# Transposing the tokens of one more tile by DMA instead of on the matrix engine

## The chip, the cores and the metric

The kernel runs on one core of a Trainium2 chip. A core has a matrix engine (TensorE, PE in the profile; its weight loads are PEld), two engines for elementwise work (VectorE, DVE; ScalarE, ACT), GpSimd (POOL) and SyncE (SP), which here only issue DMA transfers, and 16 DMA engines that move the data. Engines run in parallel, each through its own instructions in order, and wait for one another by semaphores. The metric is the time of one execution on the device in microseconds (us), the median of several runs.

## The reference, cut to what matters

Attention over 4 sequences of 768 positions with 8 heads of 64, where each position sees the first 8 positions and the last 96, with a bias that falls linearly with distance; then a two-layer network with a squared ReLU over the 3072 positions.

```python
scores = scale * np.matmul(q, k.transpose(0, 1, 3, 2))
is_global = pos[None, :] < int(n_global)             # 8
is_local = (rel >= 0) & (rel < int(n_local))         # 96
keep = is_global | is_local
scores = scores + bias[None, :, :, :]                # -slope of the head * distance
scores = np.where(keep, scores, -1000000000.0)
a = np.exp(scores - np.max(scores, axis=-1, keepdims=True))
a = a / (np.sum(a, axis=-1, keepdims=True) + 1e-09)
attn = np.matmul(a, v)
# ...
x = attn.transpose(0, 2, 1, 3).reshape(B * S, H * D)   # 3072 x 512
h = x @ w_in                                           # 512 x 2048
r = np.maximum(h, 0.0)
out = (r * r) @ w_out                                  # 2048 x 512
```

## The kernel before

The 3072 positions are 24 tiles of 128 (index `j`), two tiles to a block (12 blocks, `blk`). For each tile: q and k are transposed (`qkT`), scores are formed on TensorE (`sc`), exponentiated on ScalarE (`exp`, into `esc`), multiplied by a table of bias and mask on VectorE (`mul`, into `at`), multiplied by v on TensorE (`pv`, into `po`, two groups of four heads), and divided by the row sum on VectorE (`norm`, into `x`). For each block: x is transposed (`xT`), multiplied by eight slices of the first weights (`s1`, into `hT`), passed through ReLU on ScalarE (`relu`, into `hr`), squared on VectorE (`sq`, into `hs`) and multiplied by the second weights (`s2`, into `acc`).

The network work of some blocks is laid between the attention work of later tiles. A planner in the kernel's Python decides the order: every operation is given engines, an estimated cost, what it depends on and a priority (`key`), and the planner lists them in the order in which they would start. The program on each engine is this list. `SHIFT`, `LEADS` and `STEP` are tables of numbers that move single operations: `LEADS` moves a whole tile, `SHIFT` one kind of operation, for all tiles or for one, and `STEP` ties a tile's scores to a certain `s1` step.

The tokens of a tile are transposed in one of two ways. For tiles below `JX` it is four TensorE transposes into PSUM and a copy on VectorE or ScalarE; from `JX` on it is one DMA transpose that SyncE issues:

```python
JQK, JX = 6, 8
# ...
if j < JX:
    def emit_f(e, j=j):
        trx = ps_g.tile([P, KM, P], BF16, name="trx", tag="g")
        x = tiles["x", j].rearrange("p h d -> p (h d)")
        for kt in range(KM):                     # KM = 4
            nc.tensor.transpose(
                out=trx[:, kt, :], in_=x[:, kt * P : (kt + 1) * P], identity=ident
            )
        tiles["trx", j] = trx
    # ...
    def emit_xT(e, j=j, blk=blk, tt=tt):
        # ...
        any_copy(
            e, tiles["xT", blk][:, :, tt * P : (tt + 1) * P], tiles.pop(("trx", j))
        )
    # ...
else:
    def emit_xT(e, j=j, blk=blk, tt=tt):
        # ...
        nc.sync.dma_start_transpose(
            out=tiles["xT", blk][:, :, tt * P : (tt + 1) * P],
            in_=tiles["x", j].rearrange("p h d -> p (h d)"),
        )

    c = plan.op(("xT", j), {"SP": 1.2}, emit_xT, deps=norm, key=base + 5, takes=xT_ring)
    xop = xT_sp[j] = c
    c = plan.op(("xmoved", j), {"DMAQ": 0.9}, None, deps=[c])
```

q and k are transposed by DMA from tile `JQK` = 6 on, through the same SyncE queue as the transposes of x and the stores of the output. Their loads, issued by GpSimd, go into a ring of three buffers; the loads of tiles 8, 9 and 10 are held back by a small VectorE write to the buffer (a gate), so that they don't start too early. The gate of a tile is placed after the x transpose of the tile three before it, if that one is a DMA:

```python
if NFIRST + 2 + NQ - 1 <= j < JGATE:             # tiles 8 to 10
    def emit_gate(e, j=j):
        nc.vector.memset(qk_ring[slot(j)][:, :, :1], 0.0)

    gate = plan.op(
        ("gate", j), {"DVE": 0.07}, emit_gate, deps=qk_users[slot(j)] + [ld, xT_sp.get(j - 3)],
        key=base - 9,
    )
```

The first network weights come in eight slices of 256 columns. Slices 0 and 2 are loaded in two halves:

```python
TWO = (0, 2)
# ...
def load_w_in(s):
    n = 2 if s in TWO else 1
    for c in range(n):
        # ... one transfer of 256 / n columns
```

Of the kernel before, what the change touches and what calls it, by code (L numbers as in the profile page):

```python
# [21 lines left out]
class Plan:  # L22
# [8 lines left out]

    LAG = {"PE": 0.25, "ACT": 0.26, "DVE": 0.2, "SP": 0.6, "POOLQ": 0.8, "DMAQ": 1.2, "DMA": 0.0}
    URGE = 0.01
    SHIFT = {'T': 47, 'sc': -5.25, 'pv': -2, 'norm': 26.5, 'trx': -2, 'xT': 51, 'gk': 42, 'gv': -127.5, 'mul': 24, 'kl': 38.5, 'relu': 25.5, 'sq': 30, 's2': -5, 'o': 61, 'st': 78, ('mul', 3): 28, ('tr', 4): 10, ('xT', 5): -22, ('sc', 6): 14, ('pv', 7): -4, ('norm', 7): -17, ('trx', 7): -3, ('sc', 8): -12, ('pv', 8): -18, ('pv', 10): 45, ('sc', 11): 12, ('pv', 12): -50, ('sc', 13): 17, ('sc', 14): 6, ('pv', 14): 10, ('norm', 14): -28, ('sc', 15): -21, ('exp', 15): 20, ('exp', 16): 83, ('mul', 16): 92, ('norm', 16): -9, ('sc', 17): 32, ('pv', 17): 28, ('pv', 21): 9.5, ('pv', 22): -10, ('norm', 22): 8, ('s1', 2): -8.5, ('sq', 2): -10, ('relu', 3): 24, ('sq', 3): -82, ('s1', 5): 6, ('s1', 6): 30, ('sq', 6): 6, ('s1', 7): -6, ('sq', 7): -92, ('relu', 8): 40, ('s1', 9): -2, ('s1', 10): -10, ('s2', 0): 7.5, ('s2', 2): 1, ('s2', 4): -15, ('s2', 5): 37, ('s2', 6): -5, ('s2', 7): -3, ('s2', 9): 4.5, ('s2', 11): 30}

    def shift(self, name):
        early = name[-1 if name[0] in ("T", "tr") else 1]
        return self.SHIFT.get(name[0], 0.0) + self.SHIFT.get((name[0], early), 0.0)

# [65 lines left out]
def kernel(  # L105
# [35 lines left out]
    NFIRST = 4  # L141
    NSPLIT = 4
    NBIAS = 3
    JQK, JX = 6, 8
    NQ, NKT = 3, 2 * TPB
    NG = 8 - NACC
    G = ("g", NG)
# [7 lines left out]
    def const(shape, dt, name):  # L155
        return consts.tile(shape, dt, name=name, tag=name)
# [18 lines left out]
    pbt = const([P, 2, P], FP32, "pbt")  # L175
    pbw = const([P, 2, P], FP32, "pbw")
    plan = Plan()
    LEADS = {3: 51, 4: 17, 5: 16, 6: 27, 8: 2, 9: 20, 10: 42, 11: 47, 12: 0, 14: 0, 15: 7.5, 16: 34, 17: 46, 20: 28, 21: 15, 23: 56}
    SAFE = {j: 1.6 for j in range(6, 12)} | {14: 4.2, 15: 3.2, 16: 3.5}
    SAFEX = {9: 1.5, 11: 1.5, 13: 2.5}  # L180

# [2 lines left out]
    JOIN = {(7, 0), (12, 0), (21, 0), (16, 0), (23, 0), (18, 0), (20, 0), (15, 0)}  # L184
    COPY = [14, 15, 19, 20, 22]
    BEHIND = {}
    HOLD = ((10, 0),)
    STEP = {(4, 0): -7, (12, 0): 37, (5, 0): -2, (10, 0): 29, (13, 0): 30, (23, 1): 81}
    JGATE = 11
    NHS = 14  # L190
    NWARM = 8
# [13 lines left out]
    def slot(j):  # L205

        return j if j < NFIRST + 2 else NFIRST + 2 + j % NQ
# [60 lines left out]
    def emit_ones(e, js):  # L268
        for j in js:
            nc.vector.memset(v_sb[j][:, :, D : D + 1], 1.0)  # L270
# [38 lines left out]
    for g in range(NFIRST + 2, NT, 6):  # L309
        js = range(g, min(g + 6, NT))  # L310
        o = plan.op(
            ("ones", g), {"DVE": 0.2}, lambda e, js=js: emit_ones(e, js),
            key=-1.0, ready=15.0,
        )
# [40 lines left out]
    kl = [const([P, NPAIR, P], BF16, f"kl_{i}") for i in range(2 if COPY else 0)]  # L355
# [8 lines left out]
    for j in range(NT):  # L364
        b, t = divmod(j, TPB)
        first = t == 0
        need = 8 * (j // 2)
        base = need - LEADS.get(j, LEAD) + 4 * (j % 2)
        if (j, 0) in JOIN:
# [3 lines left out]
        if j in late:  # L373
            def emit_load(e, j=j):
                load_tile(j)
            gate = None
            if NFIRST + 2 + NQ - 1 <= j < JGATE:
# [8 lines that stand above are left out]
# [13 lines left out]
        for n in range(2) if j < JQK else ():  # L399
            users = []  # L400

            def emit_tr(e, j=j, n=n, fp=fp):
# [9 lines left out]
            tr = plan.op(  # L412
                ("tr", n, j), {"PE": 0.5 if fp else 0.24}, emit_tr,
                deps=[land["qk"[n], j]], key=base, takes=(*G, [users]),
            )
# [12 lines left out]
        if j >= JQK:  # L428
            def emit_dT(e, j=j, T_=T_):
# [5 lines left out]
            T = plan.op(  # L435
                ("T", j), {"SP": 1.3}, emit_dT,
                deps=[land["q", j], land["k", j], xT_op[j - 3]] + ku, key=base - 6,
            )
            T = plan.op(("moved", j), {"DMAQ": 1.2}, None, deps=[T])
            qk_users[slot(j)].append(T)  # L440
            if j in SAFE:

                T = plan.op(("seen", j), {"DMA": SAFE[j]}, None, deps=[T])
# [6 lines left out]
        mul, mul_users = {}, {}  # L450
# [55 lines left out]
        for gs in SETS.get(j, [tuple(range(groups))]):  # L506
            n = 8 * len(gs)
            sc_users = busers[2 * gs[0] : 2 * gs[-1] + 2]
            if (j, gs[0]) in JOIN:

                o, also, taken = joint
# [16 lines left out]
            if j < NBIAS:  # L528
# [6 lines left out]
            o = plan.op(  # L535
                ("sc", j, gs[0]), {"PE": 0.2 + 0.029 * n},
                lambda e, gs=also, f=emit_sc: f(e, gs), deps=[*deps, bias],
                key=base + 1 + 2 * gs[0], takes=takes,
            )
# [91 lines left out]
        norm = []  # L631
# [174 lines left out]
    for o in plan.ops:  # L806
        if o["name"][0] == "sc":
            j = o["name"][1]
            n = STEP.get(o["name"][1:], 4 * j - LEAD)
            if n >= 0 and j >= NFIRST:  # L810
                o["deps"].append(s1_ops[n // NSTEP, n % NSTEP])
                if o["name"][1:] in HOLD:
                    n += 1
                    s1_ops[n // NSTEP, n % NSTEP]["deps"].append(o)

    for blk in range(NBLK):
# [9 lines left out]
        for s, sub, half in order2:  # L826
# [5 lines left out]
            def emit_s2(e, blk=blk, s=s, sub=sub, half=half, w=w, cols=cols, own=own):  # L832
# [15 lines left out]
            o = plan.op(  # L848
                ("s2", blk, s, sub), {"PE": 0.43 * w / d_model}, emit_s2,
                deps=[d, land["wout", s]] + users[-1:],  # L850
                key=8 * blk + s + 2.0 + (0 if not last else 8 * sub + 8 * (half or 0)),
                takes=((*G, [users]) if own else ("acc", NACC, [users])) if s == 0 else None,
            )
# [6 lines left out]
            if s == NSTEP - 1:  # L860
# [14 lines left out]
                def emit_st(e, blk=blk, sub=sub, half=half, cols=cols):  # L875
# [9 lines left out]
                st = plan.op(  # L885
                    ("st", blk, sub), {"SP": 0.8 if (blk, sub) in HALVES else 0.4}, emit_st,
                    deps=[ev, s1_ops[NLATE, 0] if blk < NLATE - 2 else None],
                    key=8 * blk + s + 9.0,
                )
                st = plan.op(("stored", blk, sub), {"DMAQ": 1.4}, None, deps=[st])  # L890
# [40 lines left out]
```

The softmax here doesn't subtract the row's maximum and nothing guards it: scores larger than these inputs give would overflow.

## Time and profile before

| | before |
|---|---|
| time, median of three runs | 211.37 us (211.1 to 211.55) |
| span of the profiled execution | 209.3 us |
| granted TensorE clock | 1.0 |
| TensorE transposes of x (`trx`) | 32 matmuls, 8 tiles |
| copies of `trx` to `xT` | 5 on ScalarE, 3 on VectorE |
| DMA transposes of x | 16 |
| DMA transposes of q and k | 18 |

The profile numbers lines of the kernel: L709 is the TensorE transpose of x, L733 its DMA transpose, L430 the DMA transpose of q and k, L493 the scores, L646 `po`, L763 the first network layer (`hT`), L838 the second (`acc`), L880 the stores. Times in it are microseconds from the start of the span unless marked ns. A wait line names the engine and what it was about to do, then what released it, then the total, the number of waits and the longest. Matmuls are pipelined, so each one's duration overlaps the next one's; a few per cent of matmul records are missing from a trace.

### The profile page before, as it was taken

Reading aid. Unit: us, or ns where it says so; the run is one execution under the profiler, and the core shown is the slowest. Engines: PE = TensorE matmul, PEld = TensorE weight load, DVE = VectorE, ACT = ScalarE, POOL = GpSimd, SP = SyncE. Lnnn points to the kernel's source line nnn. Section 1 sums busy time; section 2 is a strip of 40 time slices with the busy share of each in tenths; the row PEclk is TensorE's granted clock in tenths of the full one; section 3 lists DMA queues with packets and bytes.
Section 4 is the critical chain, followed back from the end, with each engine's and each line's share of the span. In section 5 each row is a group of like instructions: output and inputs, shape, how many; then the busy total and the mean of one; then the engine's idle time right before and its main releaser. Section 6 shows DMA issues by size and latency. Waiting matters only on the chain.

```text
span 209.3 us, 4983 instructions
## 1 busy us (share of the span) xinstructions
PE 202.7 (97%) x1957; PEld 141.9 (68%) x1984; DVE 142.1 (68%) x370; ACT 120.2 (57%) x224; POOL 75.3 (36%) x93
## 2 busy tenths in 40 slices
PE   7998999999999999999999999999999999999994
PEld 3876887665756667676856676676676865865853
DVE  7699788523685787585958666676696865781730
ACT  6776588244872674654736564663575826841631
POOL 8999675541837057131455131313500000000000
PEclk9999999999999999999999999999999999999999
DMA  9999999999999999979999996969983421130402
GB/s 129 151 169 183 182 191 200 178 177 229 137 144 147 195 134 131 222 86 142 188 130 113 208 95 69 175 82 142 177 73 75 129 50 28 57 93 3 102 0 100
DMA packets 113705, 27.32 MB, mean 131 GB/s; under 512 B 105362, under 2 KB 110738, under 8 KB 113682
## 3 DMA queue, kind: packets, MB, share of 16 engines
q0 software_dynamic: 80256, 13.37, 85.5%
q1 hardware_dynamic: 33426, 13.64, 35.3%
q8 instruction: 15, 0.25, 0.5%
q14 instruction: 8, 0.07, 0.1%
HBM read 27.26 MB, written 6.29 MB: 160 GB/s over the span
## 4 chain that ended last, share of the span: by engine, by line
PE 88%; DVE 7%; issue 2%; ACT 2%
PE acc L838 38%; PE hT L763 37%; PE sc L493 5%; PE po L646 4%; DVE x L674 2%; PE warm L279 2%; PE tr L406 2%; ACT esc L559 1%; DVE hs L798 1%; DVE v L691 1%; DVE at L584 1%; PE trx L709 1%; DVE qkT L336 1%; DVE rs L673 1%; DVE E L343 0%
## 5 line engine op out<-in xcount | busy, mean ns | idle before, releaser
L763 PE MATMUL hT<-xT,win 128*128 128x256 bf16 x768 | 93.5, 273 | 0.4 <-DMA win<-in_moe_w_in_dram 0.4
L838 PE MATMUL acc<-wout,hs 128*128 128x512 bf16 (+2 forms) x373 | 87.1, 370 | 1.7 <-issue 0.3
L786 ACT ACTIVATE hr<-hT 128x512 f32<-128x512 f32 x96 | 57.4, 602 | 48.7 <-PE hT L763 42.9
L763 PEld LDWEIGHTS <-win 128*128 128x128 bf16 x768 | 72.8, 98 | 14.6 <-DMA win<-in_moe_w_in_dram 0.7
L798 DVE TENSOR_TENSOR hs<-hr 128x512 bf16<-128x512 f32 x96 | 64.7, 686 | 22.3 <-ACT hr L786 21.4
L838 PEld LDWEIGHTS <-hs 128*128 128x128 bf16 x400 | 36.8, 98 | 33.8
L559 ACT ACTIVATE esc<-sc 128x512 bf16<-128x512 f32 x78 | 39.9, 611 | 12.6 <-PE sc L493 12.6
L214 POOL DMA_DIRECT2D qk<-in_q_dram x23 | 20.9, 908 | 69.7 <-DMA qkT<-qk 54.8
L584 DVE TENSOR_TENSOR at<-esc,E 128x512 bf16<-128x512 bf16 x78 | 32.2, 422 | 10.4 <-ACT esc L559 7.6
L334 ACT COPY o<-acc 128x512 f32<-128x512 f32 (+2 forms) x21 | 11.6, 575 | 19.8 <-PE acc L838 19.8
L214 POOL DMA_DIRECT2D v<-in_v_dram x24 | 22.1, 922 | 1.0 <-DMA win<-in_moe_w_in_dram 0.6
L674 DVE TENSOR_TENSOR x<-po,rs 128x256 bf16<-128x256 f32 x48 | 20.4, 424 | 1.7
L214 POOL DMA_DIRECT2D qk<-in_k_dram x23 | 20.7, 911 | 0.5 <-DMA win<-in_moe_w_in_dram 0.5
L646 PEld LDWEIGHTS <-at 128*128 128x128 bf16 x352 | 15.8, 98 | 4.8 <-DVE at L584 0.2
L646 PE MATMUL po<-v,at 128*128 128x65 bf16 x352 | 17.6, 193 | 0.1
L673 DVE RECIPROCAL rs<-po 128x4 f32<-128x4 f32 x48 | 8.5, 176 | 10.8 <-PE po L646 10.3
L493 PEld LDWEIGHTS <-qkT 64*128 64x128 bf16 x312 | 9.4, 94 | 5.7 <-issue 4.9
L493 PE MATMUL sc<-qkT 64*128 64x128 bf16 x192 | 12.6, 218 | 0.0
L493 PE MATMUL sc<-qkT,qkT 64*128 64x128 bf16 x120 | 8.5, 216 | 0.0
L214 POOL DMA_DIRECT2D win<-in_moe_w_in_dram x10 | 8.1, 864 | 0.3 <-issue 0.2
L336 DVE COPY o<-acc 128x512 f32<-128x512 f32 x4 | 2.8, 692 | 6.2 <-PE acc L838 6.2
L214 POOL DMA_DIRECT2D wout<-in_moe_w_out_dram x8 | 6.0, 746 | 2.1 <-DMA win<-in_moe_w_in_dram 1.8
(45 smaller groups left out, 70.2 us busy)
## 6 DMA issues: line engine op xcount, KB each, us to landing
out_dram<-o SPq DMA_DIRECT2D x21, 256.0 KB, 3.2
v<-in_v_dram POOLq DMA_DIRECT2D x24, 128.0 KB, 5.9
qk<-in_q_dram POOLq DMA_DIRECT2D x23, 128.0 KB, 4.7
qk<-in_k_dram POOLq DMA_DIRECT2D x23, 128.0 KB, 5.3
wout<-in_moe_w_out_dram POOLq DMA_DIRECT2D x8, 256.0 KB, 9.1
win<-in_moe_w_in_dram POOLq DMA_DIRECT2D x6, 256.0 KB, 8.1
win<-in_moe_w_in_dram POOLq DMA_DIRECT2D x4, 128.0 KB, 5.1
out_dram<-o SPq DMA_DIRECT2D x4, 128.0 KB, 2.4
```

The lines of the kernel that those rows point to most:

```text
L214: nc.gpsimd.dma_start(out=dst, in_=src)
L334: nc.scalar.copy(dst, src)
L493: nc.tensor.matmul(out=tiles["sc", j, odd, g][:, at, :], lhsT=left[j - 1][half, pair, :] if kt else qkT[j % NKT][half, 1, pair, :], rhs=qk ...
L559: nc.scalar.activation(out=esc, in_=tiles.pop(("sc", j, odd, g)).rearrange("p a c -> p (a c)"), func=Act.Exp, scale=scale,)
L584: nc.vector.tensor_mul(at, tiles.pop(("esc", j, odd, g)), bias)
L646: nc.tensor.matmul(out=po[:, hi, :], lhsT=tiles["at", j, odd, g][:, at * P : (at + 1) * P], rhs=v_sb[kj][:, h, :], start=(i == 0), stop=(i ...
L673: nc.vector.reciprocal(rs, po[:, :, D : D + 1])
L674: nc.vector.tensor_tensor(out=x[:, 4 * hf : 4 * hf + 4, :], in0=po[:, :, :D], in1=rs.to_broadcast([P, 4, D]), op=Alu.mult,)
L763: nc.tensor.matmul(out=hT[:, c, :], lhsT=w_in_sb[s][:, kt, c * P : (c + 1) * P], rhs=tiles["xT", blk][:, kt, :], start=(kt == 0), stop=(kt ...
L786: nc.scalar.activation(hr, tiles.pop(("hT", blk, s)), Act.Relu)
L798: nc.vector.tensor_mul(hs, hr, hr)
L838: nc.tensor.matmul(out=tiles["acc", blk, sub, half], lhsT=hs[:, c, sub * P : (sub + 1) * P], rhs=w_out_sb[s][:, c, cols], start=(s == 0 an ...
```

## The change

Tile 7 joins the tiles whose x is transposed by DMA: `JX` goes from 8 to 7. Tile 7 is the second of block 3. The aim is to take its four transposes off TensorE and its copy off ScalarE. With this the numbers that place the operations of tiles 6 to 17 and the network blocks beside them are set anew, so that the order suits the other transpose. `TWO` is the same before and after. The loads of GpSimd keep their order.

```diff
-    SHIFT = {'T': 47, 'sc': -5.25, ... ('xT', 5): -22, ('sc', 6): 14, ('pv', 7): -4, ('norm', 7): -17, ...}
+    SHIFT = {'T': 47.0, 'sc': -5.25, ... ('xT', 5): -22.0, ('T', 6): -28.0, ('sc', 6): 6.0, ('mul', 6): -0.5, ('pv', 6): -20.5, ('norm', 6): 8.5, ...}
     # cut: some 110 entries for single operations of tiles 6 to 15 and blocks 3 to 7
...
-    JQK, JX = 6, 8
+    JQK, JX = 6, 7
...
-    LEADS = {3: 51, 4: 17, 5: 16, 6: 27, 8: 2, 9: 20, 10: 42, 11: 47, 12: 0, 14: 0, 15: 7.5, 16: 34, ...}
+    LEADS = {3: 51, 4: 17, 5: 16, 6: 49.5, 8: 140.0, 9: 30.0, 10: 27.0, 11: 48.0, 12: 14.0, 14: 0, 15: -25.5, 16: 34, ..., 7: 46.5, 13: 0.0}
...
-    HOLD = ((10, 0),)
-    STEP = {(4, 0): -7, (12, 0): 37, (5, 0): -2, (10, 0): 29, (13, 0): 30, (23, 1): 81}
+    HOLD = ((23, 1),)
+    STEP = {(4, 0): -7, (12, 0): 37, (5, 0): -2, (10, 0): 25, (13, 0): 39, (23, 1): 81, (6, 0): 17, (8, 0): 18, (9, 0): 27, (11, 0): 25, (14, 0): 35, (15, 1): 54}
```

`HOLD` names scores that the next `s1` step has to wait for in the plan.

In the programs that come out, the first 40 us of every engine are the same instructions in the same order, and so is TensorE's order after block 7. Between, the scores of tile 6 and 7 come one pair of `acc` matmuls earlier; the scores of tiles 8 to 11 come later among the network steps; the `po` groups and the network steps are moved around them. In SyncE's queue the first transpose of q and k goes ahead of the first store of the output, and tile 7's x goes between tile 8's and tile 9's transposes of q and k.

More of the change, by code (lines that the diff above doesn't have):

```diff
@@ L33 @@
     URGE = 0.01
-    SHIFT = {'T': 47, 'sc': -5.25, 'pv': -2, 'norm': 26.5, 'trx': -2, 'xT': 51, 'gk': 42, 'gv': -127.5, 'mul': 24, 'kl': 38.5, 'relu': 25.5, 'sq': 30, 's2': -5, 'o': 61, 'st': 78, ('mul', 3): 28, ('tr', 4): 10, ('xT', 5): -22, ('sc', 6): 14, ('pv', 7): -4, ('norm', 7): -17, ('trx', 7): -3, ('sc', 8): -12, ('pv', 8): -18, ('pv', 10): 45, ('sc', 11): 12, ('pv', 12): -50, ('sc', 13): 17, ('sc', 14): 6, ('pv', 14): 10, ('norm', 14): -28, ('sc', 15): -21, ('exp', 15): 20, ('exp', 16): 83, ('mul', 16): 92, ('norm', 16): -9, ('sc', 17): 32, ('pv', 17): 28, ('pv', 21): 9.5, ('pv', 22): -10, ('norm', 22): 8, ('s1', 2): -8.5, ('sq', 2): -10, ('relu', 3): 24, ('sq', 3): -82, ('s1', 5): 6, ('s1', 6): 30, ('sq', 6): 6, ('s1', 7): -6, ('sq', 7): -92, ('relu', 8): 40, ('s1', 9): -2, ('s1', 10): -10, ('s2', 0): 7.5, ('s2', 2): 1, ('s2', 4): -15, ('s2', 5): 37, ('s2', 6): -5, ('s2', 7): -3, ('s2', 9): 4.5, ('s2', 11): 30}
+    SHIFT = {'T': 47.0, 'sc': -5.25, 'pv': -2.0, 'norm': 26.5, 'trx': -2.0, 'xT': 51.0, 'gk': 42.0, 'gv': -127.5, 'mul': 24.0, 'kl': 38.5, 'relu': 25.5, 'sq': 30.0, 's2': -5.0, 'o': 61.0, 'st': 78.0, ('mul', 3): 28.0, ('tr', 4): 10.0, ('xT', 5): -22.0, ('T', 6): -28.0, ('sc', 6): 6.0, ('mul', 6): -0.5, ('pv', 6): -20.5, ('norm', 6): 8.5, ('trx', 6): 11.5, ('T', 7): 6.0, ('exp', 7): -2.0, ('gk', 7): 41.0, ('pv', 7): 24.5, ('norm', 7): 1.5, ('xT', 7): 1.0, ('gate', 8): -8.5, ('T', 8): 7.0, ('sc', 8): 3.0, ('exp', 8): -24.0, ('mul', 8): -1.0, ('gk', 8): 1.0, ('pv', 8): 127.0, ('norm', 8): 5.0, ('gv', 8): 4.5, ('xT', 8): -0.5, ('gate', 9): -6.0, ('T', 9): -6.5, ('sc', 9): -6.5, ('exp', 9): 6.0, ('gk', 9): 0.5, ('pv', 9): 5.5, ('norm', 9): 6.0, ('gv', 9): -4.5, ('xT', 9): 8.0, ('T', 10): -12.5, ('sc', 10): 3.0, ('mul', 10): -8.5, ('gk', 10): 1.0, ('pv', 10): -1.0, ('norm', 10): -5.0, ('gv', 10): -3.0, ('xT', 10): -0.5, ('T', 11): 3.5, ('sc', 11): -13.0, ('exp', 11): -10.5, ('mul', 11): -8.0, ('pv', 11): -8.0, ('norm', 11): -3.0, ('xT', 11): -5.5, ('T', 12): 1.5, ('exp', 12): -7.5, ('mul', 12): -13.0, ('pv', 12): -6.0, ('norm', 12): -0.5, ('xT', 12): 0.5, ('T', 13): -6.5, ('sc', 13): -3.0, ('exp', 13): 7.5, ('mul', 13): 0.5, ('gk', 13): -6.5, ('pv', 13): -19.5, ('norm', 13): -2.0, ('gv', 13): 13.0, ('T', 14): -9.0, ('sc', 14): 8.0, ('exp', 14): 11.5, ('mul', 14): -1.5, ('pv', 14): -28.0, ('gv', 14): 0.5, ('xT', 14): -13.5, ('T', 15): -1.5, ('sc', 15): -5.5, ('mul', 15): -11.5, ('kl', 15): -7.0, ('pv', 15): -24.5, ('norm', 15): -9.5, ('gv', 15): 3.0, ('xT', 15): -11.0, ('exp', 16): 83.0, ('mul', 16): 92.0, ('norm', 16): -9.0, ('sc', 17): 32.0, ('pv', 17): 28.0, ('pv', 21): 9.5, ('pv', 22): -10.0, ('norm', 22): 8.0, ('s1', 2): -8.5, ('sq', 2): -10.0, ('s1', 3): -3.5, ('relu', 3): 3.5, ('relu', 4): 11.5, ('sq', 4): 67.5, ('s1', 5): -7.5, ('relu', 5): 4.5, ('sq', 5): -8.0, ('s1', 6): 2.5, ('relu', 6): -6.0, ('sq', 6): 7.5, ('s1', 7): 4.5, ('relu', 7): 8.0, ('sq', 7): -54.0, ('relu', 8): 40.0, ('s1', 9): -2.0, ('s1', 10): -10.0, ('s2', 0): 7.5, ('s2', 2): 1.0, ('s2', 3): -2.0, ('o', 3): 6.0, ('st', 3): -0.5, ('s2', 4): -32.5, ('o', 4): 6.0, ('s2', 5): 18.5, ('o', 5): -15.0, ('st', 5): 19.5, ('s2', 6): 13.5, ('o', 6): -13.0, ('st', 6): -6.0, ('s2', 7): 6.5, ('st', 7): -8.5, ('s2', 9): 4.5, ('s2', 11): 30.0}
@@ L177 @@
     plan = Plan()
-    LEADS = {3: 51, 4: 17, 5: 16, 6: 27, 8: 2, 9: 20, 10: 42, 11: 47, 12: 0, 14: 0, 15: 7.5, 16: 34, 17: 46, 20: 28, 21: 15, 23: 56}
+    LEADS = {3: 51, 4: 17, 5: 16, 6: 49.5, 8: 140.0, 9: 30.0, 10: 27.0, 11: 48.0, 12: 14.0, 14: 0, 15: -25.5, 16: 34, 17: 46, 20: 28, 21: 15, 23: 56, 7: 46.5, 13: 0.0}
     SAFE = {j: 1.6 for j in range(6, 12)} | {14: 4.2, 15: 3.2, 16: 3.5}
```

## The prediction

> **What bounds the kernel now.** I read, in order: engine busy time on the page, then TensorE's waits, then busy time in four stretches after the start-up, then the chain of waits, and last the DMA transposes. The page's first part says who is full:
>
> ```profile
> span 209.3 us, 4983 instructions
> ...
> PE 202.7 (97%) x1957; PEld 141.9 (68%) x1984; DVE 142.1 (68%) x370; ACT 120.2 (57%) x224; POOL 75.3 (36%) x93
> ```
>
> TensorE is 97% busy and the next engine 68%. A pipelined matmul's duration overlaps its neighbour, so 97% is not proof; who waits is better evidence. TensorE's own waits:
>
> ```profile
> PE warm L279 <- DVE zero L267: 1.2, 1, 1.2
> PE hT L763 <- DMA win<-in_moe_w_in_dram: 0.4, 1, 0.4
> PE acc L838 <- issue: 0.3, 2, 0.2
> PE trx L709 <- DVE x L674: 0.3, 1, 0.3
> PE acc L838 <- DVE hs L798: 0.2, 1, 0.2
> PE acc L838 <- DVE qkT L620: 0.2, 1, 0.2
> ```
>
> Total, times, longest. 2.6 us in all, and the three largest fall before 20 us. By stretches (length, then PE, PEld, DVE, ACT, POOL busy):
>
> ```profile
> 20.00:50.00 30.00, 29.74 (x278) 21.96 (x283) 20.01 (x42) 17.42 (x32) 16.61 (x21) 1.00 1.72 186
> 50.00:100.00 50.00, 49.21 (x490) 33.38 (x497) 34.84 (x89) 29.40 (x56) 21.05 (x24) 1.00 1.65 154
> 100.00:150.00 50.00, 49.63 (x464) 34.63 (x469) 35.85 (x85) 28.66 (x52) 18.42 (x21) 1.00 1.29 138
> 150.00:206.50 56.50, 56.07 (x517) 39.17 (x522) 34.38 (x77) 30.00 (x55) 0.00 (x0) 1.00 0.35 66
> ```
>
> From 20 us to 206.5 us TensorE is idle for 186.5 - 184.65 = 1.85 us. Even that is mostly not idleness: the program has 400 matmuls into `acc`, the page's group has 373, and each of the 27 unrecorded ones leaves a hole of about 0.05 us ("issue" in the chain of waits below). 27 x 0.05 = 1.4 us, which leaves about 0.5 us of real waiting in 186 us. The order of this kernel has no slack left on TensorE: only fewer or cheaper TensorE instructions can shorten the middle, and any new wait lengthens it one for one.
>
> ```profile
> 57.44 0.22 PE trx L709 x4
> 57.66 0.24 PE po L646 x8
> 57.90 0.05 issue
> 57.96 0.38 PE acc L838
> 58.33 0.24 PE po L646 x8
> 58.58 1.29 PE acc L838 x6
> 59.87 0.22 PE trx L709 x4
> 60.10 0.55 PE sc L493 x16
> ```
>
> Start, length, what; this is the chain of waits around tiles 6 and 7. The second `trx` line is the work the change removes: tile 7's four transposes take 0.22 us of a full TensorE. What replaces it is a DMA transpose like those of tiles 8 to 23:
>
> ```profile
> L733 SPq DMA_TRANSPOSE xT<-x x16: 1188/1190/1211, 65.0 to 184.0; - x16
> ...
> DMA to landing us min/median/max: 2.4/2.6/4.9
> ```
>
> 1.19 us is the queue's issue time; landing takes 2.4 to 4.9 us. Asked transfer by transfer, those before 115 us, beside the loads, took 4.9, 3.8, 2.4, 4.2, 3.8 and 4.3 us; those from 132 to 150 us 2.4 to 2.7.
>
> **What the Trainium skill says.** "VectorE: DVE Perf Modes", section "The three transpose paths", gives 390 ns on TensorE and 1309 ns by DMA for one 128x128 bf16 block. The trace disagrees on what counts: one transpose shows 219 ns, but four in a stream advance TensorE by 0.22 us together, and the DMA moves four blocks with 1.19 us of issue and 2.6 us to landing. So the saving is four blocks at about 56 ns, not at 390. That 56 ns matches "TensorE: Matmul & The Clock Gate", section "Back-to-back issue gap", N/2.4 + 2.5 ns, for N = 128; the page also gives 81 ns for a sustained stream, which this trace doesn't show. "Trainium Kernel Development and Optimization", section "Key Constraints", says that DMAs issued by SyncE and GpSimd share the same 16 engines; the stretched landings beside loads agree. "Perfetto Trace Analysis", section "Identifying the Most-Contended Engine", warns against TensorE busy share as a measure; hence the waits above.
>
> **The change part by part.**
> (1) Removed: four transposes and their weight loads on TensorE, -0.22 us on the path. Also one 128x512 PSUM-to-SBUF copy on ScalarE (mean 583 ns in its group), at 57% busy: nothing on the path.
> (2) Added: one DMA transpose in SyncE's queue. No engine time; what matters is whether it lands in time.
> (3) Reordered: from TensorE's `acc` matmuls just before tile 6's scores, near 52 us, to block 7, near 130 us, instructions move by up to 2 us; later the two orders agree again. The number of separate runs of score matmuls is what could cost TensorE: entering or leaving one costs about 0.1 us (8 scores alone take 0.33 us in the chain of waits, 16 take 0.55, 24 take 0.78, so 0.028 us each and 0.1 us for the rest). Both programs have 21 such runs: 0 us. GpSimd's order of loads is the same.
> (4) Weights in halves: the first and third slices are already halved before; the text of the change names a condition, not an edit. 0 us.
> Sum: -0.22 us, plus new waits.
>
> **New waits.** I laid out the changed TensorE order at the spacings of the trace before (eight `hT` 0.87 us, two `acc` 0.43, eight `po` 0.24, scores as in (3)), and compared consumers with producers.
> - Tile 7's x. Its last `po` group should start at 57.7 us. For tile 9 before, x was ready for its DMA 1.1 us after that point (in the timeline, `po` 72.81, DMA 73.93). So the new DMA goes at 58.8, lands between 61.2 and 63.7 us; block 3's first matmul is due at 64.2. Margin 0.5 to 3.0 us: no wait, unless the SyncE queue is held by the store ahead of it, due at about 57.5.
> - Tile 9's q and k transpose now queues behind it: issued near 60.5, landing in up to 7.4 us (the longest before) by 68; its scores move from 68.6 to 70.0. No wait.
> - Tile 15's x: its last `po` group moves from 122.0 to 124.0 us, block 7 stays at 129.5. DMA at 125.1 (1.1 us after, as before: 122.0, 123.1), landing 127.5 to 129.4 with the latencies seen before 115 us, against 127.5 to 127.8 with those after 132. Margin 0.1 to 2.0 us: the tightest place. A wait of 0 to 0.5 us is possible here.
> - Others (tiles 8 to 14, 16, 17) keep distances from scores to `po` (2.7 us at least in both) and from `po` to the block's first matmul (4.7 us or more from DMA issue to use).
> I allow 0.1 us for new waits: 211.37 - 0.22 + 0.1 = 211.2 us.
>
> **Rivals.**
> - The DMA transposes collide. Tile 7's shares the DMA engines with the tail of tile 11's load (issued 55.3 to 57.9 us, about 5 us to land), tile 9's transpose and the load of tile 10, which its gate now releases about 1 us earlier. Between 36 and 72 us the engines are nearly saturated on the page (nines almost throughout). For it: `qkT` transposes there took up to 7.2 us. Against it: margins above were computed with those figures. If it bites, block 3 waits 1 to 2 us and, TensorE being full, the end moves by as much: 212 to 213.
> - TensorE transposes are hidden anyway and nothing changes. Against it: no idle time to hide them in. It would give 211.4.
> - VectorE or ScalarE becomes late, because the new order puts softmax work of two tiles close together (six exponentials in a row, about 0.5 us each, in both kernels). Some tens of 0.1 us waits would sum to 0.3 to 1 us: 211.5 to 212.2. For it: VectorE runs close behind ScalarE in that part, and a PSUM bank freed late stalls TensorE. Against it: it is so before as well, without waits.
> - More than the transposes is won, if small waits before vanish: at most the 0.5 us above, 210.7.
>
> **Range and chances.** The three runs before span 0.45 us, so a gain of 0.2 us barely shows. Downward the floor is 210.7 by the last rival; upward one missed landing costs about 1 us. Hence 210.9 to 212.2. Faster by 2% needs 4.2 us, more than TensorE's whole real idle time with the start and tail: 0.01. Slower by 2% needs several missed landings: 0.03. Within 2%: 0.96.
>
> **What would show it right or wrong.** In the profile after: 28 `trx` matmuls instead of 32, 17 DMA transposes of x, TensorE's waits after 20 us still at some tenths. A line among TensorE's waits of `hT` on the DMA `xT<-x` near 64 or 129 us would mean the landings were underestimated; waits of `sc` on `qkT<-qk`, that the queue order is at fault; waits of `po` on VectorE's `at`, that the softmax order is. The prediction is wrong if such waits sum to over 1 us, or if TensorE's saving is not about 0.2 us.

## The result, and the profile after

| | before | after |
|---|---|---|
| time, median | 211.37 us (211.1 to 211.89, 6 runs) | 212.62 us (212.13 to 213.47, 6 runs) |
| after / before | | 1.0062 [1.0035, 1.0088] |
| span of the profiled execution | 209.3 us | 210.5 us |
| end of TensorE's last matmul | 206.49 us | 207.20 us |

The change makes the kernel slower by 1.25 us; predicted was 211.2 us. The first part of the page:

```profile
span 210.5 us, 5005 instructions
...
PE 203.8 (97%) x1980; PEld 140.4 (67%) x1980; DVE 140.9 (67%) x368; ACT 121.3 (58%) x225; POOL 75.3 (36%) x93
```

TensorE's waits (total, times, longest) have one line that lies behind the start and that before doesn't have, the second:

```profile
PE warm L279 <- DVE zero L267: 1.2, 1, 1.2
PE hT L763 <- DMA xT<-x: 0.6, 1, 0.6
PE hT L763 <- DMA win<-in_moe_w_in_dram: 0.6, 2, 0.3
PE tr L406 <- DMA plain<-in_k_dram: 0.5, 1, 0.5
PE tr L406 <- DMA qk<-in_k_dram: 0.2, 1, 0.2
```

The first matmul of a network block waits for a DMA transpose of x; it is the sign that the prediction named for underestimated landings. The three below it are the loads at the start, which vary from run to run in both kernels. By stretches (length, then PE, PEld, DVE, ACT, POOL busy):

```profile
20.00:50.00 30.00, 30.00 (x282) 21.73 (x281) 18.70 (x40) 16.93 (x32) 16.72 (x21) 1.00 1.68 183
50.00:100.00 50.00, 49.35 (x492) 32.43 (x491) 35.55 (x89) 30.71 (x57) 21.03 (x24) 1.00 1.54 153
100.00:150.00 50.00, 50.00 (x469) 35.03 (x468) 34.56 (x79) 28.21 (x51) 15.79 (x18) 1.00 1.32 132
150.00:207.20 57.20, 57.20 (x526) 39.36 (x524) 35.03 (x79) 30.20 (x56) 2.63 (x3) 1.00 0.37 75
```

This trace has all 400 `acc` matmuls, so TensorE shows as full, apart from 0.65 us in the second stretch: the wait. The chain of waits there (start, length, what) names the tile:

```profile
58.30 0.19 DVE rs L673
58.50 0.02 issue
58.52 0.43 DVE x L674
58.95 0.02 SPq L733
58.98 0.03 issue
59.01 6.13 DMA xT<-x
65.14 0.04 issue
65.18 1.05 PE hT L763 x8
```

The DMA is tile 7's. Its x is ready at 58.95 us, SyncE issues at once, and 6.13 us later block 3 starts. Its eight matmuls then take 1.05 us instead of 0.87. The wait of 0.65 us and these 0.18 us together put TensorE 0.8 us later from there on than its order alone would.

The second loss lies at the very end. The last line of the chain of waits of before, and of after (start, length, what):

```profile
206.53 0.27 ACT o L334
```

```profile
207.24 0.27 ACT o L334
```

This is ScalarE's copy of the last result. From its end to the end of the span it is 209.317 - 206.792 = 2.525 us before, and 210.457 - 207.503 = 2.954 us after: 0.43 us more, in which no engine computes. The instructions of that stretch are the same in both.

### The profile page after: what moved, and what is told of

The parts are those of the page before. It is cut to its first block, busy times and chain, and to the rows that moved or that the text cites. A ratio compares the mean times of both kernels' runs of the same rounds, so it can differ in the third digit from the quotient of the medians.

```text
span 210.5 us, 5005 instructions
## 1 busy us (share of the span) xinstructions
PE 203.8 (97%) x1980; PEld 140.4 (67%) x1980; DVE 140.9 (67%) x368; ACT 121.3 (58%) x225; POOL 75.3 (36%) x93
## 4 chain that ended last, share of the span: by engine, by line
PE 84%; POOL 6%; DMA 6%; DVE 2%; issue 0%; ACT 0%; POOLq 0%; SPq 0%
PE hT L763 38%; PE acc L838 37%; PE sc L493 4%; PE po L646 4%; DMA xT<-x 3%; DMA win<-in_moe_w_in_dram 3%; POOL qk L214 3%; POOL win L214 2%; POOL v L214 2%; DVE x L674 1%; PE tr L406 0%; DVE at L584 0%; DVE hs L798 0%; DVE rs L673 0%; PE trx L709 0%
## 5 line engine op out<-in xcount | busy, mean ns | idle before, releaser
L838 PE MATMUL acc<-wout,hs 128*128 128x512 bf16 (+2 forms) x400 | 91.9, 371 | 0.0
L334 ACT COPY o<-acc 128x512 f32<-128x512 f32 (+2 forms) x23 | 12.7, 573 | 18.7 <-PE acc L838 18.4
L620 DVE COPY qkT<-qkT 128x32 bf16<-128x32 bf16 x11 | 3.3, 299 | 4.9 <-PE sc L493 4.8
```

The source lines that it names most:

```text
L334: nc.scalar.copy(dst, src)
L838: nc.tensor.matmul(out=tiles["acc", blk, sub, half], lhsT=hs[:, c, sub * P : (sub + 1) * P], rhs=w_out_sb[s][:, c, cols], start=(s == 0 an ...
```

## The experiments

Theories: A, tile 7's x lands late (A1: because tile 11's load is still in flight; A2: because of something else, such as the transpose of tile 9's q and k behind it); a rival, that something else in the new order costs time, in particular that SyncE issues the first transpose of q and k before the first store (C). Two more came from the runs: transposes of q and k land too late for the scores in the new order, in places that vary; and the longer end. Ratios are to runs of before on the same chip, with their 95% intervals; they leave out single runs that were over 1.5% slower than the fastest of their kernel, which the medians in us keep, and e17's profiled execution, which was one of them, is left out of the table and the sums below.

**e1: block 3 starts later.** `SAFEX` tells the planner how long after its DMA an x is usable; tile 7 gets an entry, and block 3's first step moves 1.3 us back in the order (as a side effect, two scores come 0.9 us earlier).

```diff
-    SAFEX = {9: 1.5, 11: 1.5, 13: 2.5}
+    SAFEX = {7: 2.5, 9: 1.5, 11: 1.5, 13: 2.5}
```

> The changed kernel with one planning number more (2.5 us of extra landing time for tile 7's x), which puts block 3's first matmuls 1.3 us later and the rest as it was; the DMA transpose stays. Theory A (the added time is TensorE's wait at about 64 us for tile 7's x, whose DMA took 6 us to land): the wait of hT on the DMA xT<-x shrinks to 0.2 us or less, the time falls to 211.2 to 211.6, ratio 0.999 to 1.001. Theory B (the new order of tiles 6 to 17 itself is the slower one): the order is nearly the same, so it stays at 212.3 to 212.9, ratio 1.005.

Measured: 211.84 us, ratio 1.0013 [0.9987, 1.0038]; no wait for x. Most of the excess is gone with the transposes' number unchanged, as A expects, though the later kernels with this edit keep more (below). Its profile does lose 0.23 us at 52.5 us, where tile 7's scores wait for their q and k.

**e2: the new order with the old transposes**, and **e3: the old order with the DMA transpose.**

```diff
-    JQK, JX = 6, 7     # e2: changed kernel
+    JQK, JX = 6, 8
-    JQK, JX = 6, 8     # e3: kernel before
+    JQK, JX = 6, 7
```

> The changed kernel's planning numbers, but tile 7 transposed on TensorE as before. Theory A: no wait of 0.5 us or more on a transpose of x before 100 us, TensorE does 0.22 us more, time 211.3 to 211.7 (ratio 0.9995 to 1.0015). Theory B (order): 212.3 or more, with waits on VectorE, ScalarE or the q and k transposes.

Measured: 222.13 us, ratio 1.0498 [1.0458, 1.0537], with waits in many places (`hT` on `xT` 2.5 us, `po` on `at` 1.6, `sc` on `qkT` 1.2).

> The kernel before with the one edit that tile 7's x goes by DMA, no new planning numbers. Block 3's first matmul stays due near 65.5 us. Theory A: the DMA is issued near 59.3 and lands by 65.4 if it again takes 6 us, so TensorE waits 0 to 0.3 us, time 211.1 to 211.6. If a DMA transpose of tile 7 costs something else (contention that delays other tiles' q, k or x), 212 or more with waits of sc on qkT<-qk.

Measured: 216.18 us, ratio 1.0232 [1.0183, 1.028]; tile 7's x causes no wait, but one of 1.4 us for the x of another tile near 129 us and others between 138 and 143 us do. Neither run splits the change into halves as meant: with the other transpose the planner lists everything behind it differently, and numbers searched for one form don't fit the other. They show only that `JX` can't be changed without a new search.

**e4: tile 11's load moved away.** A fourth tile gets the gate, so the load doesn't start before its buffer's last reader is further on.

```diff
-    JGATE = 11
+    JGATE = 12
```

> The changed kernel with a gate also for the load of tile 11, so that this load no longer runs when tile 7's x is transposed; block 3's first matmul stays due near 64.2 us. Theory A1 (the landing is stretched by the loads in flight): the DMA lands within 4 us of its issue, no wait at 64 us, time 211.1 to 211.8 unless the later load makes tile 11 wait. Theory A2 (the landing is stretched by something else, such as the q and k transpose behind it): it still takes 5.5 to 6.5 us and TensorE waits 0.5 us or more, time 212.2 or more.

Measured: 218.22 us, ratio 1.0303 [1.0267, 1.034]; as a whole much worse. Its profile has new waits near 83 us and at 131 to 135 us, for VectorE and ScalarE; that they come from the later loads is likely but not shown. What it was for is in the trace between 54 and 66 us. GpSimd's issues of loads in the changed kernel (start, length, what):

```profile
55.47 0.88 POOL L214 DMA_DIRECT2D qk<-in_q_dram  x1 [0.75 <-DMA qkT<-qk]
56.33 0.88 POOL L214 DMA_DIRECT2D qk<-in_k_dram  x1
57.20 0.90 POOL L214 DMA_DIRECT2D v<-in_v_dram  x1
```

and in e4:

```profile
53.65 0.88 POOL L214 DMA_DIRECT2D qk<-in_k_dram  x1
54.51 0.90 POOL L214 DMA_DIRECT2D v<-in_v_dram  x1
61.35 0.88 POOL L214 DMA_DIRECT2D qk<-in_q_dram  x1 [5.94 <-DVE qkT L620]
```

In the changed kernel three loads are issued in the 3.5 us before tile 7's transpose (59.01 us), in e4 the nearest is 5.2 us before it (59.70) and the next after it. The transpose ends with 32 packets of 4 bytes in the DMA records, its completion writes. In the changed kernel they come from 61.40 to 64.53 us, 2.4 to 5.5 us after the issue; in e4 all from 61.67 to 61.82, 2.0 to 2.1 us after it, and block 3 doesn't wait. The issues around the two are otherwise alike: in both, the store ahead was issued 2.52 us before and tile 9's transpose 1.3 to 1.4 us after, so A2 falls for that one. A1 holds for this place, by one profile of each: with no load in flight the transpose is done in 2 us, with the rest of a load it took 3.4 us more. In the profiles of the changed order (after, and below e6, e8, e14 and e16), all with that load close by, the last completion write came 3.5 to 5.5 us after the issue; how close the load is doesn't alone decide where in that range.

The Trainium skill, "DMA: Bandwidth & Descriptors", section "Queues, rings and completion order", says that a semaphore increment lands only after every earlier write of the same DMA engine, across its queues. No run here shows whether this delays the transpose: the records don't say which DMA engine moved a packet. It can't be all, since the data came late too: the 512 packets of 256 bytes that follow the issue moved from 1.8 to 4.5 us after it in the changed kernel, from 1.2 to 1.9 us in e4.

**e5, e6, e7: the store and the first transpose change places** in SyncE's queue: in e1's kernel, in the changed kernel, and, the other way round, in the kernel before.

```diff
-    ('T', 6): -28.0    # e5 (with e1's edit) and e6; e7 adds ('T', 6): -75 to before
+    ('T', 6): 20.0
```

> The kernel of e1 with one more swap, in SyncE's queue alone: the first store of the output goes ahead of the q and k transpose of tile 6 again, as in the kernel before. Theory C (the change has a second cost: the store between the transposes of tiles 6 and 7 lets tile 7's q and k land up to 1.25 us too late for its scores at 52 us): the tile 7 transpose is issued near 45.0 us instead of 45.6 to 46.1, no wait of sc at 52 us, the time falls by another 0.1 to 0.5 us against e1, to 211.2 to 211.6, at or just below the kernel before. Theory D (the late x was all): equal to e1, within 0.2 us.

> The changed kernel with that swap alone; block 3's first matmul stays due near 64.2 us. Theory C: the wait for tile 7's x at 64 us stays (0.4 to 0.9 us), the late q and k go: 0.1 to 0.6 us below the changed kernel on the same chip. Theory D: the same as the changed kernel.

> The kernel before with that swap in the other direction: tile 6's q and k transpose ahead of the first store, nothing else changed; tile 7 on TensorE. Its scores are 0.4 us later than in the changed kernel, so the margin is wider. Theory C: the transpose of tile 7 is issued at 45.6 to 46.1 us and lands by 51.4 to 53.6; some executions wait, median 0 to 0.4 us above the kernel before, with a wider spread. Theory D: no difference (ratio 0.999 to 1.001).

Measured: e5 212.55 us, ratio 1.0037 [1.0018, 1.0057]; e6 212.69, 1.0056 [1.0037, 1.0075]; e7 211.85, 1.0008 [0.9987, 1.0028]. C falls as the main cost: within the noise, 0.2 to 0.3%, the swap takes nothing from the changed kernel and adds nothing to before. What C names does occur, as one late landing among others: tile 7's q and k cost 0.23 us in e1's profile and 0.28 us in e14's. e6's profile shows no wait for tile 7's x, but one of 1.2 us of scores for `qkT` near 78 us: the loss isn't always in the same place.

**e8: the changed kernel once more**, to see what varies.

> The changed kernel itself, on the same chip as e5 to e7, so that they can be compared: ratio 1.003 to 1.008, spread over 1 us, with a wait for tile 7's x near 64 us that differs from the 0.65 us of its first profile by some tenths.

Measured: 212.75 us, ratio 1.005 [1.0018, 1.0082]. TensorE's waits for it:

```profile
PE sc L493 <- DMA qkT<-qk: 0.9, 1, 0.9
PE tr L406 <- DMA plain<-in_k_dram: 0.8, 1, 0.8
```

and its chain of waits from 71 us on:

```profile
71.07 8.84 DMA qkT<-qk
79.92 0.05 issue
79.96 0.62 PE sc L493 x16
```

The same kernel, but this time x is in time and the q and k transpose of tile 10 is not. It took 8.8 us. In the first profile it took 7.3 us from 70.31 and its scores started at 78.23, 0.6 us later; in before it took 7.2 from 67.39 and the scores came at 75.78, 1.2 us later. For tile 7 the distance shrank likewise from 1.4 to 0.9 us, for tile 13 from 5.0 to 0.5 us, of which 3.0 us are a longer landing (9.6 us instead of 6.6). These are the tiles whose scores can wait now.

**e9 to e12: later x, later scores of tile 10, both.** `SAFE` is for q and k what `SAFEX` is for x.

```diff
-    SAFE = {j: 1.6 for j in range(6, 12)} | {14: 4.2, 15: 3.2, 16: 3.5}
+    SAFE = {j: 1.6 for j in range(6, 12)} | {10: 3.5, 14: 4.2, 15: 3.2, 16: 3.5}   # e9, e10
     # e11: {10: 3.0, ...}; e12: {10: 2.6, ...}
-    SAFEX = {9: 1.5, 11: 1.5, 13: 2.5}
+    SAFEX = {7: 2.5, 9: 1.5, 11: 1.5, 13: 2.5}   # e9, e10, e12
     # e10 also: ('T', 6): 20.0, ('sc', 6): 14.0, the store first as in e6
```

> The changed kernel with two planning numbers more: block 3's first matmul 1.3 us later (as in e1) and tile 10's scores 0.9 us later than in the changed kernel (1.7 us later than in e1, which had moved them forward). The order of SyncE's queue is that of the changed kernel. Theory E (two landings are too late in the new order, both in the region of 60 to 80 us: tile 7's x at 64 us and tile 10's q and k at 77 us, which one bites differs from run to run): neither wait is seen in the profile; time 211.3 to 211.7, at most 0.1% above the kernel before, and the spread no wider than that of before. Theory A alone (only tile 7's x): equal to e12. If the excess sits elsewhere (start, end, tile 7's q and k): 212 or more.

> e9 with the first store of the output ahead of tile 6's q and k transpose, as in the kernel before. Theory C (late q and k of tile 7 at 52 us also cost): 0.1 to 0.4 us below e9, 211.2 to 211.5. Theory D (they do not): within 0.2 us of e9.

> The changed kernel with tile 10's scores 0.9 us later, and block 3's first matmul where it was (due at 64.2 us). Theory E: the wait at 77 us goes, that for tile 7's x at 64 us stays: 212.0 to 212.5, between e9 and the changed kernel (212.6 and 212.75). Theory A alone: no change, 212.6.

> The changed kernel with block 3's first matmul 1.3 us later and tile 10's scores where the changed kernel has them. Theory A alone: 211.3 to 211.7, as e9. Theory E: no wait for x at 64 us, but one of up to 1 us of sc on qkT<-qk near 77 us in some executions: 211.6 to 212.2.

Measured: e9 212.27 us, ratio 1.003 [1.001, 1.0049]; e10 212.24, 1.002 [1.0001, 1.0038]; e12 212.27, 1.0024 [1.0008, 1.004]; e11 213.65, 1.0104 [1.0076, 1.0131] (6 runs). e9 and e10 stay above what the theory of two late landings expected (at most 0.1%). The five kernels with later x (e1, e5, e9, e10, e12) keep 0.1 to 0.4%, on average 0.25%, whether the scores of tile 10 are moved or not; the changed kernel itself shows 0.4 to 0.6% (first result, e8, e17). The difference shows only over all of them: on one chip e5 and e8 agree within the noise. e11 is worse than expected. Its profile has the wait for tile 7's x (0.6 us) and 1.3 us of waits for the first weights at the start; the latter come before anything that the edit moves. With six runs, and after what e14 and e16 show below, it isn't evidence against later scores; it stays unexplained. e10's profile shows no late landing at all, TensorE's waits are those of the start:

```profile
PE warm L279 <- DVE zero L267: 1.2, 1, 1.2
PE tr L406 <- DMA qk<-in_k_dram: 0.3, 2, 0.2
PE hT L763 <- DMA win<-in_moe_w_in_dram: 0.3, 1, 0.3
PE trx L709 <- DVE x L674: 0.3, 1, 0.3
PE acc L838 <- DVE qkT L620: 0.2, 1, 0.2
```

and yet its end (last copy to end of span) is 2.94 us, not 2.53.

**e13 to e15: 64 or 65 DMAs on SyncE.** The tail is 2.50 to 2.53 us in before, e2 and e7, which issue 64 DMAs from SyncE, and 2.92 to 2.96 us in all kernels so far with 65. At the end SyncE checks the semaphores on which its DMAs report, one after the other in a fixed order; the DMAs take eight of them in rotation. The records of SyncE's last instructions (start in us):

```
                          before, 64 DMAs     e9, 65 DMAs
last store is issued      206.817             206.997
  it reports on           semaphore 118       semaphore 101
check of 101              207.264             208.594
         104              207.326             208.656
         105              207.390             208.720
         114              207.452             208.782
         115              207.511             208.841
         116              207.573             208.903
         117              208.037             208.962
         118              208.410             209.023
```

The last store reports about 1.6 us after its issue in both. In before it is on the last semaphore in the list, and the other checks are done while its data is under way. With one DMA more it is on 101, and seven checks of 0.06 us each follow: 209.023 - 208.594 = 0.43 us. The test is to change the number of DMAs by one without the transpose: e13 is e10 with one store left whole, e14 the changed kernel with the same, and e15 is the kernel before with one more store split.

```diff
-    HALVES = ((NBLK - 2, 0), (NBLK - 2, 1))
+    HALVES = ((NBLK - 2, 1),)                                   # e13, e14: 64 DMAs
+    HALVES = ((NBLK - 3, 0), (NBLK - 2, 0), (NBLK - 2, 1))      # e15: 65 DMAs
```

> Changed kernel with the first scores of blocks 3 and 4 moved 1.3 and 0.9 us later (as in the run before of that kind) and the store of the second to last block's last tile left whole, so that SyncE issues 64 DMAs as before the change, not 65. Tail theory (the checks of the completion semaphores at the end cost 0.43 us more with 65): the time from the end of ScalarE's last copy to the end of the span falls from 2.94 to 2.50 us, and the time by 0.43 us, to 211.8 us, ratio 1.000 (0.998 to 1.002) to the kernel before. Landing theory alone (the rest of the excess is waits for late transposes): tail 2.94, ratio 1.002 to 1.003 as without this edit.

> The changed kernel with nothing but that store left whole: 64 DMAs of SyncE. Tail theory: tail 2.50 us, 0.43 us less than the changed kernel, 212.3 us, ratio 1.003 to 1.004; the waits for tile 7's x or for a tile's qk transpose stay. Landing theory alone: tail 2.94, 212.7 us, ratio 1.005.

> The kernel before with one store more split in halves: 65 DMAs of SyncE, nothing else moved. Tail theory: tail 2.95 us where before has 2.50, +0.43 us, ratio 1.002. Landing theory alone: tail 2.50, ratio 1.000.

Measured: tails of 2.53, 2.50 and 2.94 us, all three as the number of DMAs says. e15: 212.1 us, ratio 1.0038 [1.0016, 1.0059]; the kernel before gets slower by a 65th DMA, by 0.4 us in the medians and 0.3 to 1.2 us by the interval. e13: 211.62 us, ratio 1.0001 [0.9978, 1.0024]; no excess is seen, within 0.2%. Its profiled execution had another late landing, of the x that block 8 starts with:

```profile
140.02 6.12 DMA xT<-x
```

e14: 213.68 us, ratio 1.0089 [1.0057, 1.0121] (6 runs), 1 us above what was expected. Its profile lost 1.5 us before 43 us, in waits for the first weights and k.

**e16, e17: that kernel again, beside the changed kernel itself**, on one chip.

> The changed kernel with 64 SyncE DMAs once more, beside the changed kernel with 65 on the same chip. If the earlier 213.7 us came from the slow start that its profile showed (1.5 us lost before 43 us) and not from the edit: 0.43 us below the changed kernel of the same batch, tail 2.50 us. If the edit itself costs something: again 1 us above the changed kernel.

> The changed kernel, as the partner of the run above: 212.6 to 212.8 us, ratio 1.005 to 1.006, tail 2.95 us, from the start of block 2 to TensorE's last matmul 165.6 to 166.2 us against 165.1 in the kernel before.

Measured: e16 212.08 us, ratio 1.0007 [0.9984, 1.0029]; e17 212.68 us, ratio 1.0037 [1.0016, 1.0057] (22 runs each). The version with 64 DMAs is 0.6 us below its partner, so e14's excess wasn't the edit's; why that program started slowly there is open. e14 and e16 are the same program, and their intervals don't overlap: an interval doesn't cover what differs from one occasion to the next, so small differences between ratios from different chips prove little. In e16 too transposes were late (from its chain of waits, as above):

```profile
58.83 5.59 DMA xT<-x
...
69.58 9.30 DMA qkT<-qk
...
141.19 5.02 DMA xT<-x
```

Tile 7's x, the q and k of tile 10, and the x of block 8: three transposes in the chain of waits, the two of x landing 2.6 us and more later than the 2.4 us that the fastest of their kind take.

## Why the prediction was wrong, step by step

The trace can be cut so that the start and the end fall out: from the start of block 2's first matmul, ahead of all that was reordered on TensorE, to the end of TensorE's last matmul, and from there to the end of the span. In us, for one profiled execution each:

| | from block 2 to TensorE's end | to the end of the span |
|---|---|---|
| before; e7; e15 | 165.10; 165.10; 165.10 | 2.83; 2.81; 3.25 |
| changed order: after; e6; e8; e14; e16 | 165.69; 166.15; 165.85; 165.94; 167.09 | 3.26; 3.24; 3.26; 2.80; 2.84 |
| with later scores of tile 10 alone: e11 | 165.60 | 3.26 |
| with later x: e1; e5; e9; e10; e12; e13 | 165.11; 165.24; 165.12; 164.87; 165.51; 166.86 | 3.25; 3.23; 3.24; 3.24; 3.23; 2.83 |

The old order is the same three times to the hundredth; the changed one is never twice the same.

The changed order can be taken apart. Compared step by step, executions of one order differ by more than some hundredths only where a DMA was late, by the wait and by slower matmuls right after it: 0.81 us in after, 1.27 in e6, 0.96 in e8, 1.05 in e14, 2.20 in e16, 0.23 in e1, 0.36 in e5. Taken off, 164.88 or 164.89 us remain in all seven, as in e10 (164.87), whose TensorE waits show no late landing.

- **Four transposes less, -0.22 us: right.** The changed order without late landings is 0.21 to 0.23 us under before.
- **The reordering itself, 0 us: right for TensorE's work**, by the same figures. The order costs by what it leaves to the DMAs.
- **Half a microsecond of real waiting in before: wrong, without effect.** It was left over from unrecorded matmuls. e7 has TensorE's order of before and all 400 `acc` matmuls in its trace, and TensorE is busy without a gap from 50 us to its end. So there was nothing for the rival of 210.7 us to win.
- **The added DMA: issue right, landing wrong.** Predicted: issue at 58.8, no delay by the store ahead, block 3 due at 64.2. It was issued at 59.01, with the store's issue 2.5 us ahead and not in the way. Without a wait block 3 starts 5.37 us after the issue (e4, e6, e8), as laid out. The step that failed is the landing, "between 61.2 and 63.7 us": it took the 2.4 to 4.9 us of other x transposes, and this one took 6.1 until its consumer ran. In the sum this is the 0.1 us for new waits, which came to 0.8 us in after and 2.2 us in e16. I had named the tail of tile 11's load as a neighbour, and then set the margin with transposes that didn't have one at that distance.
- **"Others (tiles 8 to 14, 16, 17) keep distances": wrong.** I had compared scores with `po` and `po` with the next block, for all tiles, but the q and k transposes with their scores only for tile 9. Those of tiles 7, 10 and 13 lost 0.5, 0.6 and 4.5 us of their margins. In before tile 10's landed with 1.2 us to spare after 7.2 us. The 9.2 and 9.3 us of e6 and e16 would have been too late there as well, but the three profiles of the old order show no such wait.
- **Tile 9's q and k, no wait: right; tile 15's x as the tightest place: not seen.** Its neighbour at 140 us, the x with which block 8 starts, was late in e13 and e16. Before leaves it 145.19 - 139.74 = 5.45 us from issue to use, after 145.04 - 140.46 = 4.58; it was among those said to keep their distance.
- **The end: not considered.** My sum ended with TensorE's last matmul. One DMA more on SyncE costs 0.43 us there, twice what the change saves.
- **Rivals.** The first, that the DMA transposes collide and give 212 to 213 us, is what happened, but its number fits partly by luck: it gave block 3 a wait of 1 to 2 us, which was 0.65 us, and 0.43 us came from the end. I gave it too little weight, because I held one execution's landings for their range. The third, VectorE or ScalarE late by the softmax order, isn't seen: TensorE's waits after the start in the changed kernel (after, e8) name DMAs alone.

Sum: -0.23 + 0.43 = +0.20 us, in each execution of the changed kernel that was profiled. The five profiles of the changed order lie on average 1.04 us above before in the middle, so late landings cost about 1.04 + 0.23 = 1.3 us, between 0.8 and 2.2. Together 1.5 us; measured by the ratios 1.3, 1.1 (e8) and 0.8 (e17). Five executions don't give that mean better than to some tenths.

Shown: the saving, the end (by adding and taking away one DMA), that the rest is late landings in varying places, and the load as the cause for tile 7's x, by e4. That waiting later for it takes back half holds on average only. Not shown: why the q and k transpose of tile 10 takes 7.2 us in one execution and 9.3 in another; I tie it to the loads only by likeness. No kernel was faster than before: e13, with both repairs, equals it within the noise. Tile 13's small margin wasn't repaired.

## What to carry to other kernels

Where one engine is full, as here, moving work from it to a DMA pays only if the DMA's slowest landing, among the neighbours that it will have, fits ahead of its consumer; one trace's maximum for that kind of transfer is not the slowest. Compare issue-to-use distances for every transfer of a reordered stretch, not only for the one that was added, and profile the same kernel more than once: a wait that moves from run to run shows a margin that is used up. And look past the last computation: count what the program has to finish before it ends.

## What the runs showed of the hardware that I had not expected

- The end of the program depends on the number of SyncE's DMAs: one more cost 0.43 us (2.50 to 2.53 us with 64, 2.92 to 2.96 us with 65, in the profiles of all 19 runs told of here), because eight semaphores are checked in a fixed order at 0.06 us each. By the table what counts is on which of the eight the last store reports, so the number of DMAs matters by its remainder by eight: an estimate from the seven checks is that a 66th would give back 0.06 us. That wasn't run.
- The same 128x512 DMA transpose reported 2.1 us after its issue without a load in flight (e4) and 5.5 us after it with one (after). The q and k transpose of tile 10 took 7.2 to 9.3 us in before, after, e8 and e16, with nothing changed ahead of it in after, e8 and e16.
